# Banded attention and a four-expert MoE on one core: when the routing probabilities are fetched, which engine makes some low halves, and where the last block's B22 lies

## The chip, the cores and the metric

The kernel runs on one core of a Trainium2 chip. A core has a matrix engine (PE; its weight loads are shown as PEld), a vector engine (DVE), a scalar engine (ACT), GpSimd (POOL) and SyncE (SP), which here does nothing but issue DMA transfers. Each engine runs its own instructions in program order and waits for others by semaphores. The metric is the device time of one execution in microseconds; less is better.

## What is computed

Only the shapes and the steps matter here. Half of the eight heads see a plain window of 32 positions, the other half every fourth position in a window of 128. The attention output, 2304 tokens by 512, goes through four experts, whose outputs are weighted by normalised probabilities:

```python
scores = scale * np.matmul(q, k.transpose(0, 1, 3, 2))      # q, k, v: (4, 8, 576, 64)
scores = np.where(masks[None, :, :, :], scores, -1000000000.0)
attn = np.exp(scores - np.max(scores, axis=-1, keepdims=True))
attn = attn / (np.sum(attn, axis=-1, keepdims=True) + 1e-09)
x = np.matmul(attn, v).transpose(0, 2, 1, 3).reshape(B * S, H * D)   # (2304, 512)
p = domain_probs / (domain_probs.sum(-1, keepdims=True) + 1e-09)     # (2304, 4)
for e in range(E):
    h = np.maximum(x @ w1[e], 0.0)           # w1: (4, 512, 1024)
    out += p[:, e:e + 1] * (h @ w2[e])       # w2: (4, 1024, 512)
```

## The kernel before

**Precision.** Every operand of an expert matmul is held as two fp32r tiles, a high half (`hi`, made by ACT, line 113) and a low half (`lo = source - hi`, made by DVE or POOL, line 116); a product is three matmuls, hi·hi, lo·hi and hi·lo (`product`, line 378). In the profile `xh`, `xl` are the halves of x, `g1h`, `g1l`, `g2h`, `g2l` those of w1, `w2h`, `w2l` those of w2, and `hh`, `hl` those of the hidden layer. `r` is a raw weight tile, `xr` raw attention output.

**Attention steps.** `steps` holds 30 attention steps: 12 with one group of queries (a head pair and a third of the sequence), then 18 with two. Iteration n of the main loop (line 702) issues several stages of different steps: the score product of step n (`s_qk`, line 264, tiles `sc`), the max of step n, the exponential of n-1, the sum and the normalisation of n-2 (line 317, POOL), the transpose of n-3 (`pt`, line 329), and the product with v of n-4 (`po`). "Step n" below means this iteration, and its start on PE is told by its score product. The loads of q, k and v for later steps are issued on SP in the same iterations, up to six groups ahead; `q7` below is the q tile of the eighth group, and so on.

**Experts.** A visit (u, m) is one 256-wide slice u of w1 and w2 on block m of 768 tokens. `visits` runs u = 1 to 15 on block 0, then all 16 slices on blocks 1 and 2 in turn. A visit's first product is a Strassen-like scheme with seven products instead of eight (`mm1_a`, `mm1_b`, lines 415 to 448); its operands from x are B11, B21, B22 and four sums of them T1 to T4. `x_sums(i)` (line 199, four DVE subtractions in place in `xr`) makes the sums of the half block i, and `x_part(i, n)` (line 209) splits one operand. `mm2` (line 462) multiplies with w2 and adds to `acc` on DVE. Slice 0 on block 0 is done by `plain` without sums; its X12 lies in the tile that T4 gets afterwards.

**What sets the order.** The order on every engine is the order in the program. Work of preparation (splits, sums) is put into the lists `queue` and `later` by `prepare`, and one item is taken (`step`) after each piece of the experts' generator; `need` takes items until a named one is done. From iteration `START` (14) on, two pieces of the experts' generator are issued in each iteration, and from `OPEN` (20) on twelve.

**Last block.** Block 2 has its own tiles for B11 and B21 only; its other operands lie in tiles of block 0 that are no longer read:

```python
    PLACE = {"T1": "B11", "B22": "B21", "T3": "T2", "T4": "T1"}
```

**Probabilities.** `weigh` (line 643) issues the DMA of the probabilities (`pw<-probs`, 128 partitions by 18 by 4 numbers) at the end of iteration 6 and normalises them with four small DVE instructions; `acc` reads them from the first `mm2` on.

Of the kernel before, what the change touches and what calls it, by code (L numbers as in the profile page):

```python
# [42 lines left out]
def kernel(  # L43
# [11 lines left out]
    nc = tc.nc  # L55
# [22 lines left out]
    pw = const.tile([128, NTT, E], F32, name="pw")  # L78
# [39 lines left out]
    def w1_split(u):  # L118

        r = raw1[u]  # L120
        gh = wp.tile([128, 3, 2, 128], F32R, tag="g1h", name="g1h", bufs=2)
        gl = wp.tile([128, 3, 2, 128], F32R, tag="g1l", name="g1l", bufs=2)
        a11, a12 = r[:, 0:2, 0:128], r[:, 2:4, 0:128]
        a21, a22 = r[:, 0:2, 128:256], r[:, 2:4, 128:256]
        for i, a in enumerate((a11, a12, a22)):
            split(gh[:, i], gl[:, i], a, nc.scalar, nc.gpsimd if u else nc.vector)
            a_op[u, ("A11", "A12", "A22")[i]] = (gh[:, i], gl[:, i])
            yield
        if u == 0:
            gh, gl = (wp.tile([128, 4, FU], F32R, tag=t, name=t) for t in ("g2h", "g2l"))  # L130
            v = (slice(None), slice(0, 2), slice(128, 256))
            split(gh[v], gl[v], a21, nc.scalar, nc.vector)
            a_op[u, "A21"] = (gh[v], gl[v])
            fetch_w1(2)
# [41 lines left out]

    PLACE = {"T1": "B11", "B22": "B21", "T3": "T2", "T4": "T1"}

    def x_op(m, n):
        if (m, n) not in b_op:
# [26 lines left out]
    def x_part(i, n):  # L209


        m, j = divmod(i, 2)
        d = {"T1": "11", "T3": "12", "T2": "22", "T4": "21"}.get(n, n[1:])
        hi, lo = (t[:, :, j * TC:(j + 1) * TC] for t in x_op(m, "T4" if n == "X12" else n))
        split(hi, lo, quarter(i, d), nc.scalar, nc.vector if i == 1 else nc.gpsimd)
        yield


# [282 lines left out]
    def experts(begin):  # L501

        for half in range(2):
            for n in ("X12", "B22") if half else ("B11", "B21"):
                for i in range(2):
                    need(x_part, i, n)
            need(w1_split, 0)
            yield from plain((0, 0), half)
            if half == 1:
                for n in ("T4", "T3", "T1", "T2"):  # L510
                    for j in (1, 0):
                        prepare(x_part, j, n, soon=True)
                prepare(w1_late, 1, soon=True)
                prepare(w1_split, 2)
                prepare(w1_sums, 2)
            need(w2_late, 0)
            yield from mm2((0, 0), True, False, half)
            if half == 0:
                yield from pause("open")
            else:  # L520
                prepare(w2_late, 2)
        need(w1_split, 1)
        yield from mm1_a(visits[0])
        for i, (u, m) in enumerate(visits):
            blocks = [b for v, b in visits if v == u]
            mine = [v for v in visits if v[1] == m]
            ends = m and (u, m) == mine[0], (u, m) == mine[-1]
            if m == blocks[0]:
                need(w1_late, u)
            need_x(m)  # L530
            yield from mm1_b((u, m))
            if m == blocks[-1] and u < LAST:
                prepare(w1_late, u + 1)
            if (u, m) == (NU - 1, 0):
                need(x_sums, 4)
                need(x_sums, 5)
                for n in ("T2", "T1", "T3", "T4"):
                    for j in (4, 5):
                        prepare(x_part, j, n)
            if m == blocks[-1] and u + 2 <= LAST:  # L540
                prepare(w1_split, u + 2)
                prepare(w1_sums, u + 2)
            if m == blocks[0]:
                need(w2_late, u)
            yield from mm2((u, m), *ends, 1)
            if i + 1 < len(visits):
                begin()
                need(w1_split, visits[i + 1][0])
                need_x(visits[i + 1][1], ("B11", "B21"))
                yield from mm1_a(visits[i + 1])  # L550
                if visits[i + 1] == (NU - 1, 0):

                    for j in (4, 5):
                        prepare(x_part, j, "B22")
                    for j in (4, 5):
                        prepare(x_sums, j)
            yield from mm2((u, m), *ends, 0)
            if m == blocks[-1] and u + 2 <= LAST:
                prepare(w2_late, u + 2)
# [27 lines left out]
    with tc.manual_schedule():  # L587
# [38 lines left out]
        def begin():  # L626

            if "over" in gate and "m1" not in gate:
                gate.add("m1")
                early.close()  # L630
                pools["x"] = ctx.enter_context(
                    tc.tile_pool(name="x2", bufs=1, side="right", reuse_waits="tile")
                )
                for n, bufs in ("m1", 2), ("m2", 4):
                    pools[n] = ctx.enter_context(
                        tc.tile_pool(name=n, bufs=bufs, space=psum, reuse_waits="tile")
                    )
                pools["acc"] = pools["x"]
                for n in ("B11", "B21"):
                    for i in (4, 5):  # L640
                        prepare(x_part, i, n)

        def weigh():

            nc.sync.dma_start(out=pw, in_=probs.rearrange("(t p) e -> p t e", p=128))
            nc.vector.reduce_sum(out=ps_, in_=pw, axis=mybir.AxisListType.X)
            nc.vector.tensor_scalar(
                out=ps_, in0=ps_, scalar1=1e-9, scalar2=None, op0=ALU.add
            )
            nc.vector.reciprocal(out=pr_, in_=ps_)  # L650
            nc.vector.tensor_tensor(
                out=pn, in0=pw, in1=pr_.to_broadcast([128, NTT, E]), op=ALU.mult
            )
# [34 lines left out]
        for n, i, names in (  # L688
            (done(*plains[0]), 0, ("B11",)), (done(*plains[0]), 1, ("B11",)),
            (START - 1, 0, ("B21",)), (START - 1, 1, ("B21",)),  # L690
            (done(*dil(0, 1)), 0, ("X12", "B22", None)),
            (OPEN - 1, 1, ("X12", "B22", None)),
            (done(*dil(1, 1, 2)), 2, X_PARTS), (done(*dil(2, 0, 1)), 3, X_PARTS),
        ):
            when.setdefault(n, []).append((i, names))
# [6 lines left out]
        for n in range(len(steps) + LAG):  # L702
# [15 lines left out]
            for i, names in when.get(n, ()):  # L718
                for name in names:
# [1 line left out]
                    if name is None or name == "T2":  # L721
                        prepare(x_sums, i, of=of)
                    if name is not None:
                        prepare(x_part, i, name, of=of)
            if n == 2:
                fetch_w1(0)
                fetch_w2(0)
                fetch_w1(1)
            if n == 4:
                prepare(w1_split, 0)  # L730
                prepare(w2_late, 0)
            if n == 6:
                weigh()
            if n == 8:
                prepare(w1_split, 1)
# [81 lines left out]
```

## Time and profile before

| what | value |
|---|---|
| time, median of 3 runs (lowest to highest) | 878.15 us (878.09 to 879.53) |
| time of the profiled execution | 878.14 us |
| span of its trace, first to last instruction | 876.4 us |
| PE busy | 843.3 us, 96% of the span |
| DVE, POOL, ACT busy | 494.3, 430.3, 328.5 us |
| mean granted clock of PE | 0.986 |

The trace covers the span; 1.74 us of the profiled execution lie outside it. The engine names, the times from the start of the span and the idle time ahead of an instruction (with what ended it, in brackets) are read from the rows further below. A busy PE is not PE at full speed: the granted clock is either 1.0 (2.4 GHz) or 0.5 (1.2 GHz), and a mean between them is a stretch that holds both.

### The profile page before, as it was taken

To read this page: it belongs to the slowest core of one execution; us is meant where nothing else is said; L and a number is where in the kernel's file an instruction comes from. 1 tells how busy PE (TensorE), PEld (TensorE's weight loads), DVE (VectorE), ACT (ScalarE), POOL (GpSimd) and SP (SyncE) were. 2 spreads that over 40 slices of the span, in tenths; PEclk is the share of its full clock that TensorE was granted. 3 is DMA by queue.
4 is the path that set the end of the run, shared out by engine and by line. 5 is a ranking of instruction groups with operands and counts; after the bars stand their busy time and mean duration, and the time that the engine had idled before them with its cause. 6 is when DMAs were issued, how large, how long until landed. Compare 5 with 4: busy or idle time off the path is not lost.

```text
span 876.4 us, 13448 instructions
## 1 busy us (share of the span) xinstructions
PE 843.3 (96%) x5096; PEld 734.6 (84%) x5096; DVE 494.3 (56%) x1029; ACT 328.5 (37%) x771; POOL 430.3 (49%) x508
## 2 busy tenths in 40 slices
PE   8598899999999999899999999999999999999998
PEld 5477678888788988688898988989889898898987
DVE  3577766567565565745555555554555545555454
ACT  4354544445344444433333333422333332343221
POOL 4574887678876677954224323423422432342310
PEclk9699999999999999999999999999999999999999
DMA  7754123322222211230101001001110100100003
GB/s 229 185 161 127 47 87 112 109 83 82 76 62 86 73 49 51 74 117 26 48 25 49 25 25 49 24 25 48 29 44 25 49 24 25 49 25 25 1 25 120
DMA packets 54528, 56.77 MB, mean 65 GB/s; under 512 B 5952, under 2 KB 43840, under 8 KB 54464
## 3 DMA queue, kind: packets, MB, share of 16 engines
q1 hardware_dynamic: 54464, 55.92, 20.7%
q8 instruction: 40, 0.66, 0.3%
q14 instruction: 24, 0.20, 0.1%
HBM read 51.19 MB, written 4.72 MB: 64 GB/s over the span
## 4 chain that ended last, share of the span: by engine, by line
PE 85%; DVE 6%; POOL 5%; issue 1%; ACT 1%; DMA 1%; SPq 0%; POOLq 0%; DVEq 0%; ACTq 0%
PE m L480 42%; PE m1x L382 21%; PE m1y L382 16%; DVE hl L406 3%; PE pt L329 2%; PE sc L264 2%; DVE xr L204 2%; PE po L349 1%; POOL xl_T L116 1%; POOL sm L294 1%; POOL g1l L116 1%; PE wt L675 1%; POOL sm L317 1%; DVE u L442 1%; DMA q_s<-qT 1%
## 5 line engine op out<-in xcount | busy, mean ns | idle before, releaser
L489 DVE SCALAR_TENSOR_TENSOR acc<-m,pn,acc 128x512 f32<-128x512 f32 x270 | 201.9, 749 | 103.1 <-PE m L480 101.7
L480 PE MATMUL m<-w2h,hh 128*128 128x512 f32 x576 | 227.5, 395 | 7.6 <-DVE acc L489 7.1
L480 PE MATMUL m<-w2h,hl 128*128 128x512 f32 x576 | 229.4, 398 | 2.4 <-DVE hl L406 0.9
L116 POOL TENSOR_TENSOR g2l<-r,g2h 128x256 fp32r<-128x256 f32 x124 | 91.7, 761 | 280.0 <-ACT g2h L113 279.9
L480 PE MATMUL m<-w2l,hh 128*128 128x512 f32 x576 | 226.9, 394 | 0.0
L480 PEld LDWEIGHTS m<-w2h,hl 128*128 128x128 f32 x576 | 108.6, 189 | 36.0 <-DVE hl L406 13.6
L480 PEld LDWEIGHTS m<-w2h,hh 128*128 128x128 f32 x576 | 108.7, 189 | 30.9 <-DVE acc L489 10.1
L480 PEld LDWEIGHTS m<-w2l,hh 128*128 128x128 f32 x576 | 108.7, 189 | 20.0
L116 POOL TENSOR_TENSOR w2l<-r,w2h 128x512 fp32r<-128x512 f32 x62 | 80.1, 1309 | 46.0 <-ACT w2h L113 45.6
L438 DVE TENSOR_TENSOR s<-m1x,s 128x384 f32<-128x384 f32 x47 | 26.2, 558 | 109.0 <-PE m1x L382 106.2
L419 ACT ACTIVATE s<-m1x 128x384 f32<-128x384 f32 x47 | 23.1, 491 | 171.4 <-PE m1x L382 171.4
L116 POOL TENSOR_TENSOR g1l<-r,g1h 128x256 fp32r<-128x256 f32 x93 | 69.0, 756 | 35.0 <-ACT g1h L113 34.8
L400 ACT ACTIVATE hh<-s 128x384 fp32r<-128x384 f32 x94 | 49.4, 526 | 97.3 <-DVE s L438 50.8
L431 ACT ACTIVATE u<-m1x 128x384 f32<-128x384 f32 x47 | 23.1, 491 | 149.7 <-PE m1x L382 149.7
L406 DVE SCALAR_TENSOR_TENSOR hl<-s,hh 128x384 fp32r<-128x384 f32 x94 | 59.4, 632 | 30.1 <-ACT hh L400 30.0
L382 PE MATMUL m1x<-xh_T,g2h 128*128 128x384 f32 x188 | 63.8, 339 | 1.5 <-ACT u L431 1.5
L382 PE MATMUL m1x<-xl_T,g2h 128*128 128x384 f32 x188 | 63.4, 337 | 0.0
L382 PE MATMUL m1x<-xh_T,g2l 128*128 128x384 f32 x188 | 63.3, 337 | 0.0
L422 DVE TENSOR_TENSOR s<-m1y,s 128x384 f32<-128x384 f32 x47 | 26.2, 557 | 61.4 <-PE m1y L382 57.1
L113 ACT ACTIVATE g2h<-r 128x256 fp32r<-128x256 f32 x125 | 44.6, 405 | 0.0
L382 PE MATMUL m1y<-xh_B,g2h 128*128 128x384 f32 x128 | 43.0, 336 | 0.0
L382 PE MATMUL m1y<-xl_B,g2h 128*128 128x384 f32 x128 | 42.9, 336 | 0.0
(86 smaller groups left out, 1548.3 us busy)
## 6 DMA issues: line engine op xcount, KB each, us to landing
r<-w SPq DMA_DIRECT2D x64, 512.0 KB, 3.5
v_s<-vw SPq DMA_DIRECT2D x48, 144.0 KB, 3.3
k_s<-kT SPq DMA_DIRECT2D x48, 112.0 KB, 3.2
q_s<-qT SPq DMA_DIRECT2D x48, 96.0 KB, 3.2
out<-acc SPq DMA_DIRECT2D x18, 256.0 KB, 2.1
mask<-masks SPq DMA_DIRECT2D x1, 288.0 KB, 3.2
pw<-probs SPq DMA_DIRECT2D x1, 36.0 KB, 3.3
```

Of the source, the lines that this page charges most:

```text
L113: nc.scalar.activation(out=hi, in_=src, func=AF.Copy)
L116: lo_eng.tensor_tensor(out=lo, in0=src, in1=hi.bitcast(F32), op=ALU.subtract)
L204: nc.vector.tensor_tensor(out=quarter(i, d), in0=quarter(i, a), in1=quarter(i, b), op=ALU.subtract)
L382: nc.tensor.matmul(bank, w[:, k], x[:, k], start=(first and k == 0 and i == 0), stop=(last and k == 1 and i == 2), skip_group_check=True,)
L400: nc.scalar.activation(out=hi, in_=src, func=AF.Relu)
L406: nc.vector.scalar_tensor_tensor(out=lo, in0=src, scalar=0.0, in1=hi.bitcast(F32), op0=ALU.max, op1=ALU.subtract)
L419: nc.scalar.activation(out=s1, in_=x, func=AF.Copy)
L422: nc.vector.tensor_tensor(out=s1, in0=z, in1=s1, op=ALU.add)
L431: nc.scalar.activation(out=u2, in_=x, func=AF.Copy)
L438: nc.vector.tensor_tensor(out=s5, in0=x, in1=s5, op=ALU.add)
L480: nc.tensor.matmul(po, a[:, i * 128:(i + 1) * 128], w, start=(n == 0), stop=(n == 5))
L489: nc.vector.scalar_tensor_tensor(out=acc, in0=po, scalar=pn[:, tt, e:e + 1], in1=acc, op0=ALU.mult, op1=ALU.add,)
```

## The change

1. The DMA of the probabilities moves from the end of iteration 6 to the end of iteration 2, right behind the first three weight loads; the four DVE instructions move to the end of iteration 11.
2. The low halves of w1's slice 1 (three, iterations 8 to 10) go from POOL to DVE.
3. The low halves of x go to DVE for every odd half block (i = 1, 3, 5), where before only i = 1 did.
4. T2, T1 and T3 of half block 0 are queued in iteration 15, ahead of X12 and B22 of half block 1, instead of after `plain`.
5. Block 2 gets a tile of its own for B22. Its T2 lies in block 0's B11 and its T1 in block 0's B21. B11, B21, B22 and the sums of block 2 are queued in `later` as soon as the attention is over, T2 and T1 one visit later, T3 and T4 last.

```diff
-            split(gh[:, i], gl[:, i], a, nc.scalar, nc.gpsimd if u else nc.vector)
+            split(gh[:, i], gl[:, i], a, nc.scalar, nc.gpsimd if u > 1 else nc.vector)
...
-    PLACE = {"T1": "B11", "B22": "B21", "T3": "T2", "T4": "T1"}
+    PLACE = {"T2": "B11", "T1": "B21", "T3": "T2", "T4": "T1"}
...
-        split(hi, lo, quarter(i, d), nc.scalar, nc.vector if i == 1 else nc.gpsimd)
+        split(hi, lo, quarter(i, d), nc.scalar, nc.vector if i % 2 else nc.gpsimd)
...
-                for n in ("T4", "T3", "T1", "T2"):
-                    for j in (1, 0):
+                for n, js in (("T4", (1, 0)), ("T3", (1,)), ("T1", (1,)), ("T2", (1,))):
+                    for j in js:
                         prepare(x_part, j, n, soon=True)
...
             if (u, m) == (NU - 1, 0):
-                need(x_sums, 4)
-                need(x_sums, 5)
-                for n in ("T2", "T1", "T3", "T4"):
+                for n in ("T3", "T4"):
                     for j in (4, 5):
                         prepare(x_part, j, n)
...
                 if visits[i + 1] == (NU - 1, 0):
-                    for j in (4, 5):
-                        prepare(x_part, j, "B22")
-                    for j in (4, 5):
-                        prepare(x_sums, j)
+                    need(x_sums, 5)
+                    for n in ("T2", "T1"):
+                        for j in (4, 5):
+                            prepare(x_part, j, n)
...
-                for n in ("B11", "B21"):
+                for n in ("B11", "B21", "B22"):
                     for i in (4, 5):
-                        prepare(x_part, i, n)
+                        prepare(x_part, i, n, of=later)
+                for i in (4, 5):
+                    prepare(x_sums, i, of=later)
...
-            nc.sync.dma_start(out=pw, in_=probs.rearrange("(t p) e -> p t e", p=128))
             nc.vector.reduce_sum(out=ps_, in_=pw, axis=mybir.AxisListType.X)
...
-            (done(*dil(0, 1)), 0, ("X12", "B22", None)),
+            (done(*dil(0, 1)), 0, ("X12", "B22", None, "t2", "t1", "t3")),
...
-                        prepare(x_part, i, name, of=of)
+                        prepare(x_part, i, name.upper(), of=of)
             if n == 2:
                 fetch_w1(0)
                 fetch_w2(0)
                 fetch_w1(1)
+                nc.sync.dma_start(out=pw, in_=probs.rearrange("(t p) e -> p t e", p=128))
...
-            if n == 6:
+            if n == 11:
                 weigh()
```

PE's instructions keep their order and number; only the names of the tiles that block 2 reads differ. Three places on other engines carry the argument.

On SP, early in the attention, before the change the probabilities stood behind the loads of iteration 6, ahead of the weight tile of slice 2 (`r_465`):

```order
L247 DMA k_s<-kT 128x224
L252 DMA v_s<-vw 96x2x192
L645 DMA pw<-probs 128x18x4
L246 DMA q_s<-qT 128x192
L247 DMA k_s<-kT 128x224
L252 DMA v_s<-vw 96x2x192
L98 DMA r_465<-w 128x4x256
```

With the change they stand behind the three weight loads of iteration 2, ahead of q7 and k7:

```order
L98 DMA r_231<-w 128x4x256
L106 DMA r_233<-w 128x2x512
L98 DMA r_235<-w 128x4x256
L728 DMA pw<-probs 128x18x4
L246 DMA q_s<-qT 128x192
L247 DMA k_s<-kT 128x224
L246 DMA q_s<-qT 128x192
```

So the transfer moved past fourteen loads of q, k and v, which now stand behind it.

On ACT, at the opening of the second half of `plain`, before the change the splits of X12 (`xh_T_0_905`) and B22 (`xh_B_0_919`) of half block 1 came right after an exponential:

```order
L336 ACTIVATE pts<-pt 96x384
L302 ACTIVATE sm_95<-sm_95 128x6x96
L113 ACTIVATE xh_T_0_905<-xr 128x2x192
L113 ACTIVATE xh_B_0_919<-xr 128x2x192
L400 ACTIVATE hh<-m1x 128x384
```

With the change the high halves of T2, T1 and T3 of half block 0 stand ahead of them:

```order
L302 ACTIVATE sm_95<-sm_95 128x6x96
L113 ACTIVATE xh_T_0_1298<-xr 128x2x192
L113 ACTIVATE xh_T_0_1302<-xr 128x2x192
L113 ACTIVATE xh_T_0_1306<-xr 128x2x192
L113 ACTIVATE xh_T_0_905<-xr 128x2x192
L113 ACTIVATE xh_B_0_919<-xr 128x2x192
L400 ACTIVATE hh<-m1x 128x384
```

Their three POOL low halves move likewise, ahead of the four `g2l` of slice 1.

On DVE, in the visits (14, 0) and (15, 0), before the change the eight sums of block 2 stood in one piece behind the hidden layer's low halves and ahead of three additions to `acc`:

```order
L438 TENSOR_TENSOR s_4306<-m1x,s_4306 128x384
L442 TENSOR_TENSOR u_4305<-m1y,u_4305 128x384
L406 SCALAR_TENSOR_TENSOR hl<-s_4306,hh 128x384
L406 SCALAR_TENSOR_TENSOR hl<-u_4305,hh 128x384
L406 SCALAR_TENSOR_TENSOR hl<-m1x,hh 128x384
L204 TENSOR_TENSOR xr<-xr 128x2x192 x8
L489 SCALAR_TENSOR_TENSOR acc_989<-m_4376,pn,acc_989 128x512
```

With the change they stand one visit earlier, one or two at a time between the visit's own instructions, and three low halves of B11, B21 and B22 (`xl_B`) stand just ahead of them on DVE:

```order
L116 TENSOR_TENSOR xl_B_2_4154<-xr,xh_B_2_4153 128x2x192
L204 TENSOR_TENSOR xr<-xr 128x2x192
L438 TENSOR_TENSOR s_4158<-m1x,s_4158 128x384
L204 TENSOR_TENSOR xr<-xr 128x2x192
L442 TENSOR_TENSOR u_4157<-m1y,u_4157 128x384
L406 SCALAR_TENSOR_TENSOR hl<-s_4158,hh 128x384
L406 SCALAR_TENSOR_TENSOR hl<-u_4157,hh 128x384
L204 TENSOR_TENSOR xr<-xr 128x2x192
L406 SCALAR_TENSOR_TENSOR hl<-m1x,hh 128x384
L204 TENSOR_TENSOR xr<-xr 128x2x192
L489 SCALAR_TENSOR_TENSOR acc_989<-m_4219,pn,acc_989 128x512
```

The sums are spread, and two of them now stand ahead of the hidden layer's work in this visit.

## Rows read from the trace of the kernel before

**Rows 1.** Timeline of PE: start us, us, instruction, idle before and its releaser.
```profile
29.62 0.87 PE L329 MATMUL pt<-ident,sm 128*96 128x128 f32 x3 [7.68 <-POOL sm L317]
...
75.40 0.44 PE L382 MATMUL m1x<-xh_T,g1h 128*128 128x384 f32 x1 [1.15 <-ACT xh_T L113]
...
229.32 0.50 PE L480 MATMUL m<-w2h,hh 128*128 128x512 f32 x1 [1.53 <-DVE acc L489]
...
369.02 0.79 PE L480 MATMUL m<-w2h,hh 128*128 128x512 f32 x1 [3.64 <-DVE acc L489]
```

**Rows 2.** Timeline of DVE around the probabilities (columns as above).
```profile
26.83 0.23 DVE L646 TENSOR_REDUCE ps__69<-pw 128x18 f32<-128x72 f32 x1 [6.65 <-DMA pw<-probs]
...
28.09 0.45 DVE L310 TENSOR_REDUCE su<-sm 128x3 f32<-128x291 f32 x1
...
29.23 0.61 DVE L116 TENSOR_TENSOR g2l<-r,g2h 128x256 fp32r<-128x256 f32 x1
```

**Rows 3.** Timeline of PE: score products of steps 7, 13 and 14.
```profile
20.51 0.71 PE L264 MATMUL sc<-k_s,q_s 64*64 64x96 f32 x12
...
44.07 0.73 PE L264 MATMUL sc<-k_s,q_s 64*64 64x96 f32 x24
...
47.45 1.24 PE L264 MATMUL sc<-k_s,q_s 64*64 64x96 f32 x24
```

**Rows 4.** Tile k_s, the one transfer (k7) issued at 13.04 us.
```profile
DMA to landing us min/median/max: 6.9/6.9/6.9
```

**Rows 5.** Windows: busy us of PE, PEld, DVE, ACT, POOL; clock; DMA share, GB/s.
```profile
25.00:26.50 1.50, 0.00 (x0) 0.00 (x0) 0.00 (x0) 0.00 (x0) 0.00 (x0) 0.50 0.92 48
47.50:51.00 3.50, 3.50 (x33) 3.28 (x33) 2.47 (x15) 1.88 (x5) 3.07 (x3) 0.53 0.47 131
333.50:348.90 15.40, 15.40 (x79) 13.96 (x78) 8.15 (x13) 7.58 (x18) 12.73 (x16) 1.00 0.11 35
```

**Rows 6.** Groups by line of DVE, 26 to 36 us: busy us, mean ns.
```profile
L116 DVE TENSOR_TENSOR w2l<-r,w2h 128x512 fp32r<-128x512 f32 x2 | 1.8, 918 | 0.0
```

**Rows 7.** Waits of SP's queue, 0 to 45 us: total us, times, longest.
```profile
SPq L98 <- DVE g2l L116: 2.9, 1, 2.9
...
SPq L252 <- DMA r<-w: 1.3, 1, 1.3
```

**Rows 8.** Timeline of SP: issues of v5, q12, w1 slice 2, k15.
```profile
19.40 0.57 SPq L252 DMA_DIRECT2D v_s<-vw  x1
...
24.16 1.62 SPq L246 DMA_DIRECT2D q_s<-qT  x1
...
29.87 0.38 SPq L98 DMA_DIRECT2D r<-w  x1
...
36.34 0.42 SPq L247 DMA_DIRECT2D k_s<-kT  x1
```

**Rows 9.** Tile k_s, the one transfer (k15) issued at 36.34 us.
```profile
DMA to landing us min/median/max: 3.9/3.9/3.9
```

**Rows 10.** Timeline of ACT: four high halves of x in a row.
```profile
90.18 1.75 ACT L113 ACTIVATE xh_T<-xr 128x384 fp32r<-128x384 f32 x4
```

**Rows 11.** Waits of all engines, 97 to 102 us: total us, times, longest.
```profile
PE m L480 <- DVE hl L406: 0.7, 2, 0.4
```

**Rows 12.** Timeline of POOL: an attention step's subtraction behind low halves.
```profile
225.74 1.15 POOL L294 TENSOR_TENSOR sm<-sm,nm 128x576 f32<-128x576 f32 x1
```

**Rows 13.** Timeline of DVE: `s` of visit (14, 0); the eight sums of block 2.
```profile
339.61 0.56 DVE L438 TENSOR_TENSOR s<-m1x,s 128x384 f32<-128x384 f32 x1 [2.46 <-PE m1x L382]
...
358.97 9.33 DVE L204 TENSOR_TENSOR xr<-xr 128x384 f32<-128x384 f32 x8
```

**Rows 14.** Critical chain, merged: start us, us, what.
```profile
369.02 5.49 PE m L480 x12
...
396.26 4.12 PE m L480 x18
```

**Rows 15.** Line 204, all sums: duration ns min/median/max.
```profile
L204 DVE TENSOR_TENSOR xr<-xr x24: 543/964/1534, 61.2 to 367.3; 128x384 f32<-128x384 f32 x24
```

## The prediction

> **What bounds the kernel.** PE is busy for 96% of the span and the change leaves its instructions as they are, so I add up nothing but time in which PE stood still or ran at the lower clock. The timeline of PE gives the idle places. The largest is 7.68 us ahead of a transpose in step 8 and the next 3.64 us ahead of an `mm2` of block 0; smaller ones lie where `plain` opens its second half and near 229 us [rows 1]. For each the reader should ask which instruction came last, and follow that engine's own timeline back.
>
> The first one is a wait for data. DVE stood 6.65 us for `pw<-probs`, with the sums of the next attention step queued behind [rows 2]; POOL's normalisation and PE's transpose followed. Steps 7 to 14 therefore took from 20.51 to 47.45 us, 26.94 us [rows 3].
>
> **The change part by part.**
>
> *Probabilities.* The wait goes, since by iteration 11 the transfer has long landed. What is late next? Three things.
>
> First, k7. The transfer now stands ahead of it, in a queue that was already slow: k7 landed 6.9 us after its issue at 13.04, at 19.9 us [rows 4], 0.6 us before step 7 used it. The probabilities come in runs of 16 bytes. In the 1.5 us from 25.0 the DMA engines were 0.92 busy and moved 48 GB/s, 72 KB, of which the probabilities are 36 [rows 5]. Between half of that stretch and all of it, 0.7 to 1.5 us, is their price; I take 1.3, as the rate shows them to fill most of it. k7 then lands at 21.2, and step 7 starts at about 21.3 instead of 20.5.
>
> Second, DVE. A step's own work there is 1.14 us, from its sum at 28.09 to the next low half at 29.23 [rows 2]; five steps, 7 to 11, make 5.7. Added in these steps are two `w2l` at 0.92 [rows 6], so 1.8; one `g2l` and the three `g1l` that come over from POOL at no more than 0.61 each, 2.4; and the four normalising instructions with one more `g1l`, 26.83 to 28.09, 1.3 [rows 2]. Together 11.2 us, and step 12 starts at 32.5. If all of it were hidden, the steps would go at PE's pace. The row nearest to that is step 13 to 14, 3.4 us with two groups, or 1.7 for one [rows 3]; five make 8.5, and step 12 starts at 29.8. I take the sum, because DVE is in order and every step needs its reciprocal.
>
> Third, SP. v5 is the eighth transfer behind w1's slice 1, and its issue at 19.40 waited 1.3 us for a weight load [rows 7, 8]; I read this as at most eight transfers in flight. With the change v5 is the eighth behind the probabilities, so it waits until these land, at about 20.6, 1.2 us later than before, with every later load behind it. Slice 2 of w1 was ready to be issued at 29.87 less a wait of 2.9 for its buffer [rows 7, 8], at 27.0; with the change DVE frees that buffer in time. Add 1.2; take off the probabilities' own issue, 0.6, and the 1.1 us by which q12 behind them was slower than a common issue (1.62 against 0.57) [rows 8]: 26.5. From there to the landing of k15 it took 6.5 us of issues and 3.9 us of transfer [rows 8, 9], so k15 lands at 36.9. Step 13 needs it; the engines would be there by 32.5 plus at most 3.4, 35.9. So the loads bind: step 13 at 36.9, step 14 one spacing of 3.4 later, at 40.3 instead of 47.45. **Gain 7.2 us.** Without this bind it is 8.2; with DVE's work hidden too, 10.9. Step 14 ran at clock 0.53 for 3.5 us [rows 5], which cost some 1.6 us; PE has as many gaps ahead of it with the change, so I leave that as it is, and take 5 us as the lower end (price of the probabilities 0.2 more, and another slow stretch of 1.6 us or so).
>
> *T2, T1 and T3 of half block 0 earlier.* ACT has three high halves more ahead of X12, at 0.44 each [rows 10], 1.3 us. PE had been waiting for just that one, 1.15 us [rows 1]. PE's first two matmuls need no low half and cover a little of DVE's; I take a loss of 1.2 us. Later the same three are missing where ACT, DVE and POOL are crowded, at 88 to 102 us; but the chain there (sum, high half, four splits, copy on ACT) keeps its length, and I count only the two waits for `hl`, 0.7 us [rows 11], since POOL comes to the attention's subtraction earlier. **Loss 0.5 us**; from a loss of 1.2 to a gain of 1.
>
> *Low halves of half block 3 on DVE.* The wait of 1.53 us at 229.32 [rows 1] ends a chain: POOL got to the attention step's subtraction at 225.74 only [rows 12], behind low halves; ACT's exponential and `hh` behind it were late, and so `hl` and `acc`. POOL loses seven instructions ahead of it, so the wait goes. DVE takes them, between its additions. **Gain 1.5 us**, 0 to 2.
>
> *Last block.* The eight sums held DVE for 9.33 us, 1.17 each [rows 13], with three `acc` queued behind; PE ran out of PSUM and stood 3.64 us [rows 1], and then its twelve matmuls took 5.49 us, where eighteen take 4.12 at full clock [rows 14], so 2.75: 2.7 lost to the clock. Both go, 6.3 us. In their place stand eleven DVE instructions in visit (14, 0). Before, DVE was busy there for 8.15 of 15.40 us, PE without a gap [rows 5]. A sum takes 0.54 us at least and 0.96 in the median [rows 15]. At 0.54 eleven take 5.9 and fit into the 7.2 us that are free; at 1.17 they take 12.9, and 5.6 us do not fit. POOL is at work for 12.73 of the 15.40 us [rows 5], and so I price them by the slow row.
>
> The excess is not all PE's. Only the instructions that stand ahead of `s`, `u` and the first `hl` hold it back; those behind delay `acc`, for which four PSUM tiles give slack, and `s` of the next visit, whose `hl` is needed ten us later. Counting along the order: ahead of `s` now stand three low halves and a sum, 3.8 us at the median price and 4.7 at the slow one. `s` had 2.46 us of idle time right ahead of it [rows 13], and between the additions DVE had about one more (an estimate out of the 7.2): `s` is 0.3 to 1.2 late, I take 0.8. One sum more, 1.2, stands ahead of `u` and the two `hl`. PE waits some 2.0 us in two or three pieces, all short. **Gain 4.3 us**; from -0.3 (all the excess, and one us more) to 6.3.
>
> The row shows 1.17 for a sum beside a busy POOL against 0.54 at best [rows 13, 15]. The Trainium skill, "SBUF — State Buffer", section "Who interferes with whom", says that a DVE instruction with two SBUF inputs and a GpSimd instruction that reads SBUF exclude each other for the whole of the earlier one's time; the trace agrees with alternation. By it the moved low halves would cost DVE a POOL instruction's time each, which speaks against this part of the change, and the sum would be that of the third rival below.
>
> *The rest.* The tile of its own for B22 and the new places cost nothing that I can see: block 0's B11 and B21 are last read in the visit before T2 and T1 are written, and PE's order is the same. If T2 came late, PE would wait in visit (16, 2), over 25 us later; that is its cover.
>
> **Sum.** 7.2 - 0.5 + 1.5 + 4.3 = 12.5 us. The profiled execution took 878.14 us, 1.74 of it outside the span, and equals the median (878.15): 878.1 - 12.5 = 865.6 us. Its own range is 862 to 869.
>
> **The rivals.**
>
> *The loads do not bind.* If eight in flight is a misreading, or the issues catch up, the early gain is 8.2 to 10.9. For it: SP had idle time before most of these loads. Against it: the landings above. 864.6 to 861.9 us, some 862.5.
>
> *DVE is too full.* In the last block all 5.6 us of the excess reach PE, and the three `hl` there slow down by 0.5 each: 6.3 less 7.1, -0.8. The early part and the rest stay: 878.1 - 7.2 + 0.5 - 1.5 + 0.8 = 870.7. For it: 1.17 in the row; against: `acc` has slack.
>
> *The stall only moves.* The step that loses its wait starves for q and k in steps 8 to 13, and 3 of 7.2 us remain: 869.8. For it: 0.6 us of slack at k7. If nothing at all were left of the early gain (the change doesn't do what it says), 872.8.
>
> *Slower.* Each moved instruction costs what the worst sum did, 1.53 us [rows 15]: eleven make 16.8 in visit (14, 0), 9.6 more than fit, and with `hl` 11 us and a new slow stretch of 2.7; seven make 10.7 near 215 us and cost 4 instead of gaining 1.5. Then 878.1 - 7.2 + 0.5 + (11 + 2.7 - 6.3) + 4 = 882.8. It decides once DVE costs PE over 14 us in both places together (the early gain, and the two waits that go). Against it: that price occurred once in 24.
>
> **How the numbers follow.** My forecast 0.55; loads do not bind 0.17; DVE too full 0.15; the stall only moves 0.09, slower 0.03; 0.01 is left. The range 861 to 871 takes in the first, most of the second, half of the third and most of the fourth (0.55, 0.15, 0.08, 0.07), 0.85; cut at 869 it would leave out 0.3. About 0.2% (1.8 us) is what a measurement of this kernel can tell from no change. Faster by more than that: the first four, 0.95; same 0.02; slower 0.03.
>
> **What would show it.** In the profile after: no wait of DVE for the probabilities; step 7 near 21.3 and step 14 near 40.3; the issue of v5 right after the probabilities land, and step 13 starting as k15 lands (a wait for a load at PE, or none, decides between forecast and first rival). A longer wait for `xh_T` where `plain` opens its second half. No wait near the old 229. No slow clock after visit (14, 0), but waits of PE for `hl` in it, 2 us in all; over 5 us there would be the third case. I am wrong if PE's idle time early in the attention is as long as before, or if a new stretch at the lower clock shows up.

## The result, and the profile after

| what | before | after |
|---|---|---|
| median time (lowest to highest), 4 executions each | 878.12 us (876.96 to 879.53) | 868.04 us (866.52 to 869.99) |
| ratio to before, 95% interval | | 0.9886 (0.986 to 0.9911) |
| profiled execution: span | 876.4 us | 866.9 us |
| mean granted clock of the executions | 0.986 (profiled) | 0.987 to 0.995 |

The change gained 10.1 us where 12.5 were forecast; the time lies inside the range. PE executes the same 5096 matmuls in the same order in both kernels, so the start of the k-th matmul in one trace less its start in the other says how much is **in hand** at that place. Step 12's score product, for example, began at 41.33 us before and at 34.17 after: 7.2 us in hand. The table gives this at eleven places, named by their time in the trace of before.

| place, us before | 20.5 (step 7) | 41.3 (step 12) | 47.5 (step 14) | 74 | 88 | 115 | 130 | 324 | 365 | 393 | end |
|---|---|---|---|---|---|---|---|---|---|---|---|
| in hand, us | -1.5 | 7.2 | 5.6 | 5.5 | 1.2 | 3.5 | 3.0 | 3.8 | 2.6 | 9.2 | 9.5 |

The wait of 7.68 us is gone, but two stretches give back what it brought: steps 13 and 14, and the ten microseconds behind 74. The timeline of PE after (columns as in [rows 1, 3]) has the places:

```profile
17.50 0.57 PE L349 MATMUL po<-pts,v_s 96*64 96x64 f32 x12 [2.26 <-ACT pts L336]
...
22.03 1.17 PE L264 MATMUL sc<-k_s,q_s 64*64 64x96 f32 x12
...
34.17 0.73 PE L264 MATMUL sc<-k_s,q_s 64*64 64x96 f32 x24
...
36.91 0.38 PE L264 MATMUL sc<-k_s,q_s 64*64 64x96 f32 x4
...
39.33 0.71 PE L264 MATMUL sc<-k_s,q_s 64*64 64x96 f32 x20 [2.04 <-DMA k_s<-kT]
...
41.86 1.24 PE L264 MATMUL sc<-k_s,q_s 64*64 64x96 f32 x24
...
71.11 0.69 PE L382 MATMUL m1x<-xh_T,g1h 128*128 128x384 f32 x1 [2.39 <-ACT xh_T L113]
...
216.07 0.49 PE L480 MATMUL m<-w2h,hh 128*128 128x512 f32 x1 [0.80 <-DVE acc L489]
...
225.57 0.50 PE L480 MATMUL m<-w2h,hh 128*128 128x512 f32 x1 [0.33 <-DVE acc L489]
...
337.66 0.44 PE L382 MATMUL m1x<-xh_T,g1h 128*128 128x384 f32 x1 [0.92 <-DVE s L438]
```

Step 7 starts at 22.03 and its product takes 1.17 us, the duration of the lower clock. Step 13 starts at 36.91, does four matmuls and waits 2.04 us for k15. Where `plain` opens its second half the wait for `xh_T` has grown from 1.15 [rows 1] to 2.39 us. In the last block nothing is left of the 3.64 us of [rows 1]; 0.92 us ahead of `s` is new.

SP's timeline after shows why the loads are late (issues of the probabilities, q7, v5 and k15; columns: start, duration of the issue):

```profile
12.47 0.51 SPq L728 DMA_DIRECT2D pw<-probs  x1
13.08 5.97 SPq L246 DMA_DIRECT2D q_s<-qT  x1
...
22.38 0.57 SPq L252 DMA_DIRECT2D v_s<-vw  x1
...
33.96 0.42 SPq L247 DMA_DIRECT2D k_s<-kT  x1
```

Right behind the probabilities one issue takes 5.97 us, where a common one takes about half a microsecond [rows 8]. SP does not wait for a landing here, it stands inside the issue, and everything behind starts from 19.05. (The view of SP's waits puts 5.0 us of it down to PE's product with v at 17.50; but in `contig` below, with the same order on PE, this issue was through at 14.6, ahead of that product, so it is no wait for PE.) The tile view of k15 (`k_s`, issued at 33.96) puts its landing at 39.2:

```profile
DMA to landing us min/median/max: 5.2/5.2/5.2
```

And in the windows of after (columns as in [rows 5]) the clock is low at 40 to 47 and at 70 to 78 us, and full behind the last block's old wait:

```profile
40.00:47.00 7.00, 7.00 (x54) 5.87 (x52) 5.47 (x30) 3.63 (x8) 5.64 (x5) 0.51 0.68 190
70.00:78.00 8.00, 6.36 (x20) 5.86 (x21) 5.45 (x8) 1.48 (x4) 3.45 (x3) 0.57 0.23 63
330.00:345.00 15.00, 14.03 (x70) 12.09 (x69) 14.06 (x20) 7.34 (x19) 14.58 (x15) 1.00 0.12 37
366.00:376.00 10.00, 9.94 (x50) 8.47 (x49) 6.88 (x10) 3.96 (x9) 7.81 (x10) 1.00 0.38 130
```

### The profile page after: what moved, and what is told of

Same layout as the page of the kernel before. It is cut to its first block, busy times and chain, and to the rows that moved or that the text cites. A ratio compares the mean times of both kernels' runs of the same rounds, so it can differ in the third digit from the quotient of the medians.

```text
span 866.9 us, 13453 instructions
## 1 busy us (share of the span) xinstructions
PE 842.7 (97%) x5096; PEld 734.4 (85%) x5096; DVE 503.9 (58%) x1046; ACT 328.7 (38%) x771; POOL 417.6 (48%) x491
## 4 chain that ended last, share of the span: by engine, by line
PE 87%; DVE 6%; POOL 2%; ACT 2%; DMA 2%; issue 1%; SPq 0%; POOLq 0%; DVEq 0%; ACTq 0%
PE m L480 44%; PE m1x L382 22%; PE m1y L382 17%; DVE hl L406 2%; PE sc L264 1%; PE pt L329 1%; PE po L349 1%; DVE xr L204 1%; PE wt L674 1%; DVE sm L278 1%; DVE u L442 1%; DMA r<-w 1%; DMA k_s<-kT 1%; ACT hh L400 1%; POOL xl_T L116 0%
## 5 line engine op out<-in xcount | busy, mean ns | idle before, releaser
L116 POOL TENSOR_TENSOR g1l<-r,g1h 128x256 fp32r<-128x256 f32 x90 | 66.7, 756 | 36.4 <-ACT g1h L113 36.4
L382 PE MATMUL m1x<-xh_T,g2h 128*128 128x384 f32 x156 | 52.8, 339 | 0.6 <-ACT u L431 0.3
L382 PE MATMUL m1x<-xl_T,g2h 128*128 128x384 f32 x156 | 52.5, 337 | 0.2 <-DVE xl_T L116 0.2
L382 PE MATMUL m1x<-xh_T,g2l 128*128 128x384 f32 x156 | 52.3, 335 | 0.0
```

The source lines that it names most:

```text
L116: lo_eng.tensor_tensor(out=lo, in0=src, in1=hi.bitcast(F32), op=ALU.subtract)
L382: nc.tensor.matmul(bank, w[:, k], x[:, k], start=(first and k == 0 and i == 0), stop=(last and k == 1 and i == 2), skip_group_check=True,)
```

## The experiments

All times are medians of 4 to 6 executions, ratios are to the kernel before on the same chip. One program's executions differ by 1 to 5 us, and go with their mean granted clock: `warm` below took 865.25 us at 0.998 and 870.06 at 0.986. A time alone therefore settles little under 2 us; the traces are read for the places. Four theories were at stake: that part 4 costs the clock at 71 to 77 us (A), that the probabilities' many runs hold SP (B), that the clock and not the wait is what part 4 costs (C), and that an old wait for w1's load starts the lower clock of the early attention (D).

**Parts alone or undone.** `late_t` undoes part 4 in the changed kernel:

```diff
-            (done(*dil(0, 1)), 0, ("X12", "B22", None, "t2", "t1", "t3")),
+            (done(*dil(0, 1)), 0, ("X12", "B22", None)),
...
-                for n, js in (("T4", (1, 0)), ("T3", (1,)), ("T1", (1,)), ("T2", (1,))):
-                    for j in js:
+                for n in ("T4", "T3", "T1", "T2"):
+                    for j in (1, 0):
```

> The changed kernel with part 4 undone: T2, T1 and T3 of half block 0 are queued after plain again. Theory A: the three high halves ahead of X12 make PE wait 2.39 instead of 1.15 us at 71 us, and with that its clock falls to 0.5 until 77; of the 5.5 us in hand at 70 us only 3.2 are left at 118. Undone: wait about 1.2 us, clock 1.0 from 71 to 77, 5.0 to 5.5 us in hand there and 1 to 2 of them lost again at 86 to 98, where the waits of before return. Time 864.5 to 866.5 us. Rival: the lower clock has to do with the earlier arrival of the whole stretch (DVE, POOL and loads in another phase), not with part 4; then it stays and the time is 868 to 869 us.

Measured 867.81 us, 0.9878 (0.9863 to 0.9893): like the changed kernel. In its windows the stretch at 70 to 78 us is at full clock, as theory A said, but a new one stands at 88 to 95, behind the two waits in the PE rows below it:

```profile
24.00:43.00 19.00, 19.00 (x200) 13.43 (x200) 11.36 (x64) 9.12 (x24) 11.74 (x16) 0.50 0.84 238
70.00:78.00 8.00, 5.74 (x43) 4.62 (x36) 6.05 (x22) 3.27 (x8) 1.78 (x3) 1.00 0.29 75
88.00:95.00 7.00, 6.27 (x60) 5.13 (x60) 3.49 (x6) 3.69 (x10) 6.92 (x8) 0.52 0.00 0
```

```profile
85.93 0.41 PE L382 MATMUL m1y<-xh_T,g2h 128*128 128x384 f32 x1 [0.98 <-DVE s L422]
...
88.73 0.69 PE L382 MATMUL m1x<-xh_T,g2h 128*128 128x384 f32 x1 [1.52 <-ACT u L431]
```

Part 4 shortens these two waits (to 0.48 and 0.31 us in the trace of after) and lengthens one at 71; each way one piece at half clock is paid. From 74 to 115 us `late_t` lost 1.0 us of what it had in hand, the changed kernel 2.1. The first window shows a second thing: here PE ran at half clock from 24 to 43 us without a gap (19.00 of 19.00 us busy), and only 3.4 us were in hand at step 14.

`probs_alone` is the kernel before with part 1 alone:

```diff
-            nc.sync.dma_start(out=pw, in_=probs.rearrange("(t p) e -> p t e", p=128))
             nc.vector.reduce_sum(out=ps_, in_=pw, axis=mybir.AxisListType.X)
...
                 fetch_w1(1)
+                nc.sync.dma_start(out=pw, in_=probs.rearrange("(t p) e -> p t e", p=128))
...
-            if n == 6:
+            if n == 11:
```

> The kernel before with part 1 alone (fetched in iteration 2, normalised in iteration 11). If the early gain belongs to part 1 alone: step 14 at 41.5 to 42 us, 5.5 us in hand at 70 us, no clock of 0.5 from 71 to 77 (theory A), waits at 86 to 98, 229 and 369 us as before: 872 to 873 us. Rival: the stretch at 0.5 comes with the earlier arrival and not with part 4: 875 to 876 us.

Measured 872.89 us, 0.9941 (0.9927 to 0.9955), so 5.2 us for part 1. Both readings were half right: no low clock at 71 to 77, but the one at 88 to 95 (0.52), as in `late_t`. In hand at 74 us were 4.2, at 115 us 3.2. In the last block the wait stood as before, in this PE row, but the clock stayed at 1.00 behind it, as the window says, where it fell to half before ([rows 14]: 5.49 us for twelve):

```profile
366.17 0.50 PE L480 MATMUL m<-w2h,hh 128*128 128x512 f32 x1 [3.60 <-DVE acc L489]
```

```profile
366.00:376.00 10.00, 9.68 (x47) 8.27 (x47) 7.58 (x13) 6.43 (x15) 9.31 (x11) 1.00 0.78 262
```

`last_alone` is the kernel before with part 5 and the low halves of half block 5 on DVE (`i in (1, 5)`).

> The kernel before with part 5 alone and the low halves of half block 5 on DVE; everything up to 330 us as before. If the gain of the last block is independent of the rest: wait of 3.64 us and the lower clock at 369 us gone, waits of about 1.5 us for s and hl in visit (14, 0), net 5 us: 873 to 873.5 us. By the prediction 4.3 us: 874. Rival: part of it depended on the other parts (POOL freed of low halves): 875 us or more.

Measured 874.23 us, 0.9955 (0.9941 to 0.9969), 4.0 us; in its trace, which is of its fastest execution (872.43 us), nothing was in hand at 324 us, -1.1 at 365, 5.6 at 393. The gain does not need the other parts. Its cost is the wait for `s`:

```profile
341.39 0.44 PE L382 MATMUL m1x<-xh_T,g1h 128*128 128x384 f32 x1 [0.92 <-DVE s L438]
```

`half3_pool` puts only the low halves of half block 3 back on POOL (`i in (1, 5)` for `i % 2` in the changed kernel).

> The changed kernel with the low halves of half block 3 on POOL again (those of half block 5 stay on DVE). As predicted, 1.5 us are lost by it: 869.5 us. By the trace of the changed kernel the wait at 229 shrank from 1.53 to 0.33 us, but one of 0.8 came at 216 where there had been 0.25, so 0.6 us: 868.6 us. Rival: it is neutral, 868.0 us.

Measured 870.82 us, 0.9907 (0.9891 to 0.9924). The intervals overlap, the early clock differs too, and the trace is of its fastest execution (868.43 us), so I go by the place: from 130 to 324 us the changed kernel wins 0.8 us and this one 0.1. Its waits are those of before:

```profile
214.62 0.51 PE L480 MATMUL m<-w2h,hh 128*128 128x512 f32 x1 [0.24 <-DVE acc L489]
...
225.33 0.50 PE L480 MATMUL m<-w2h,hh 128*128 128x512 f32 x1 [1.52 <-DVE acc L489]
```

`p2_pool` puts the low halves of w1's slice 1 back on POOL (`u > 1` to `u`).

> The changed kernel with the low halves of w1's slice 1 on POOL again. By the prediction DVE's own work sets the pace of steps 7 to 12, and the three low halves are 1.8 us of it; k15 binds behind it: step 12 about 1.5 us earlier than 34.2, steps 13 and 14 where they are, time unchanged at 868 us. Rival: POOL sets the pace (PE's waits in these steps are for its normalisation): steps 8 to 12 are later by 1 to 2 us, and the time is 868.5 to 869.5 us.

Measured 870.05 us, 0.9901 (0.9886 to 0.9915). Inconclusive: PE ran at half clock here without a gap, so neither DVE nor POOL set the pace, as this window shows:

```profile
20.00:38.00 18.00, 18.00 (x167) 12.79 (x164) 9.39 (x53) 9.23 (x25) 11.86 (x18) 0.50 0.85 239
```

**SP and the probabilities.** `fetch_4` moves the fetch, the DMA line alone, from `n == 2` to the end of iteration 4.

> The changed kernel with the probabilities' DMA at the end of iteration 4 instead of 2, the normalisation stays in iteration 11. Theory B: behind three weight loads that are still in flight the transfer of 2304 runs of 16 bytes holds SP, whose next issue took 5.97 us, and so k7, step 7 and at last k15 are late. In iteration 4 the weights have nearly landed: no issue over 2 us, step 7 at about 20.5 instead of 22.0 us, k15 lands at 37 to 38 instead of 39.2, and the time is 1 to 2 us less, 866 to 867 us. Rival: the same bytes and runs stand ahead of the later loads in any case; SP catches up by step 13, k15 lands at 39 and the time stays at 868 us.

Measured 867.07 us, 0.9867 (0.9854 to 0.9881). SP's rows:

```profile
20.20 0.60 SPq L729 DMA_DIRECT2D pw<-probs  x1
20.89 1.22 SPq L246 DMA_DIRECT2D q_s<-qT  x1
```

The issue behind it takes 1.22 us, PE waits for a load only once, 0.45 us, and 6.1 us are in hand at step 14. Step 7 was not earlier (22.87): PE's clock was already low there, behind a wait of 2.21 us at 17.7 for ACT.

`contig` leaves the fetch in iteration 2 and changes the layout in memory only:

```diff
-                nc.sync.dma_start(out=pw, in_=probs.rearrange("(t p) e -> p t e", p=128))
+                nc.sync.dma_start(out=pw, in_=probs)
...
-        "probs": moe_domain_probs[rows], "w1": moe_w1, "w2": moe_w2,
+        "probs": moe_domain_probs[rows].reshape(-1, 128, E).transpose(1, 0, 2), "w1": moe_w1, "w2": moe_w2,
```

> The changed kernel with one thing different: the probabilities lie in memory partition by partition, so that the same 36 KB come as 128 runs of 288 bytes instead of 2304 runs of 16; place and time of the fetch are those of the changed kernel. Theory B (the number of runs holds SP): the next issue takes under 1.5 us instead of 5.97, k7 lands near 20 us, no wait of PE for a load at 20 to 24 us, k15 lands 1 to 2 us earlier than 39.2; 866 to 867 us. Rival (three weight loads of 512 KB hold the queue whatever stands behind them): the next issue still takes 5 to 6 us and the time stays at 868 us.

Measured 868.07 us, 0.9882 (0.987 to 0.9895). On SP the rival falls:

```profile
12.45 1.57 SPq L728 DMA_DIRECT2D pw<-probs  x1
14.12 0.51 SPq L246 DMA_DIRECT2D q_s<-qT  x1
```

0.51 us in place of 5.97: the number of runs held SP, behind the same three weight loads. The other traces repeat it: the issue behind the probabilities took 4.71 to 6.54 us in the six kernels that fetch 2304 runs in iteration 2, and 0.38 to 0.75 in the four that fetch 128. k15 was issued at 31.21 and landed 5.0 later, at 36.2; step 14 began at 40.49, with 7.0 us in hand. The Trainium skill, "DMA: Bandwidth & Descriptors", section "Rules for kernel authors", says that a last dimension that is not contiguous becomes one descriptor per element, and advises rearranging it. Here the last dimension was contiguous, for 16 bytes, so that advice does not reach this case; the trace shows that short runs cost the queue too. Yet the median did not move. In hand at 115 us were 4.9, behind the same stretch at half clock from 69 to 77 us.

**The clock.** `warm` gives PE work where it stood still:

```diff
             need(w1_split, 0)
+            if half == 1:
+                dummies(20)
             yield from plain((0, 0), half)
```

> The changed kernel with twenty extra matmuls (bf16, 256 columns, into a PSUM tile that nothing reads) ahead of the second half of plain, where PE stood still for 2.39 us at 68.7 to 71.1. They compute nothing of the result. Theory C: the wait for xh_T itself costs only 1.2 us more than before, and the rest of what is lost from 70 to 78 us (another 2.5 to 3) is the lower clock that follows it; with PE at work in the wait the clock stays at 1.0, the first product of the half starts at the same 71.1, and 2 to 3 us are gained: 865 to 866 us. Rival: the clock falls in spite of it (the stretch ahead is busy enough to lower it), or falls some us later, at the waits near 87 us: 868 us.

Its PE rows and the window around the place:

```profile
67.42 3.33 PE L676 MATMUL wt<-ident 128*128 128x256 bf16 x20
70.50 0.42 PE L382 MATMUL m1x<-xh_T,g1h 128*128 128x384 f32 x1
```

```profile
69.00:77.00 8.00, 7.11 (x39) 5.52 (x37) 6.80 (x9) 3.14 (x8) 3.81 (x4) 1.00 0.14 38
```

The clock stays at 1.0, and nothing falls later: from 74 to 115 us 0.2 us are won where the changed kernel lost 2.1. So theory C holds for this place, and the other traces bear it out: all six kernels with part 4 and without these matmuls have the wait of 2.39 us and a stretch at half clock behind it, and lose 1.2 to 2.3 us from 74 to 115; the four with them have no such stretch and win 0.2. The median, 868.29 us, 0.9883 (0.9867 to 0.99), does not show it: the profiled execution took 865.25 us at a mean clock of 0.998, the four others 867.0 to 870.1 at 0.986 to 0.992. Where these lost theirs isn't in a trace; in the other kernels' traces the place that varies most is 17 to 50 us.

`split6` takes away the wait that seemed to start that early stretch, in `contig`:

```diff
-            if n == 4:
+            if n == 6:
                 prepare(w1_split, 0)
                 prepare(w2_late, 0)
```

> The kernel with the probabilities in 128 runs, and the splits of w1's and w2's slice 0 queued in iteration 6 instead of 4. Theory D: in all kernels so far ACT stands some 3 us for w1's load (g1h, landing at 16 to 17.5 us) ahead of an attention step's copy, PE waits 1.0 to 3.0 us for it at 17 us, and that wait starts the lower clock at 18 to 24 us, in some executions to 38; whether it does is what makes the executions of one kernel differ by 3 us. Without the wait: no idle of PE over 0.7 us at 17, clock 1.0 from 16 to 36, step 7 at 20 us or earlier; median 865.5 to 867 us, mean clock of the executions 0.991 or more. Rival: the splits come later and hold DVE in steps 9 to 12, or the clock falls there for another wait: 868 us, mean clocks as before.

Measured 870.16 us, 0.9912 (0.9898 to 0.9926). Theory D falls in its consequence: the wait at 17 us is gone, but PE then overtakes the loads, and at the opening of `plain` it waits for a high half of x, which on ACT stands behind an exponential that had itself waited 1.61 us for POOL:

```profile
19.87 1.14 PE L264 MATMUL sc<-k_s,q_s 64*64 64x96 f32 x12 [1.65 <-DMA k_s<-kT]
...
42.90 0.44 PE L382 MATMUL m1x<-xh_B,g1h 128*128 128x384 f32 x1 [2.44 <-ACT xh_B L113]
```

Each is followed by a stretch at half clock; 9.8 us were in hand near 38 us and 5.0 at 58.

`combo` adds the extra matmuls to `split6`.

> The kernel with all three: probabilities in 128 runs, splits of slice 0 in iteration 6, and twenty extra matmuls ahead of the second half of plain (they compute nothing of the result). If the two stretches at the lower clock (17 to 40 us, 70 to 78 us) are what is lost of the early gain, both are gone: clock 1.0 up to 100 us but for some 3 us near 42, 7 to 8 us in hand at 118 us, mean clock 0.995 or more in every execution, 862 to 864 us. Rival: a stretch at the lower clock appears elsewhere in its place (87 to 95 us): 866 to 868 us.

Measured 868.52 us, 0.9891 (0.9874 to 0.9908): the rival in kind, at other places than it named. The clock was at 1.0 from 70 to 78 us, but at 0.57 from 32 to 40 and 0.53 from 43 to 50. Against `split6` it is 1.6 us less, with intervals that overlap.

`contig_warm` and `f4_warm` keep the splits in iteration 4 and combine the extra matmuls with either remedy for SP.

> The changed kernel with the probabilities in 128 runs and the twenty extra matmuls (they compute nothing of the result); the splits stay in iteration 4. If the two gains add up (k15 some 3 us earlier, no lower clock at 70 to 78 us): 7 us in hand at 70 us and 6.5 at 118, a span of about 862.5 us and a median of 864 to 866 us. Rival (what is gained in one place is lost at the next, as the two runs before showed): 867 to 868.5 us.

> The changed kernel with the fetch in iteration 4 and the twenty extra matmuls (they compute nothing of the result). Fetch in iteration 4 alone gave 867.1 us with mean clocks of 0.990 to 0.992 in every execution, of which the stretch at 70 to 78 us is part; without that stretch 864.5 to 866 us. Rival: 867 us or more, because the stretch comes later or the clock of the early attention varies more than it did in those four executions.

`contig_warm` took 867.98 us, 0.9876 (0.9861 to 0.9892); `f4_warm` 865.44 us (864.71 to 865.93), 0.9851 (0.9838 to 0.9865), the best here, with mean clocks of 0.994 to 0.997 in all five executions. Against the same kernels without the extra matmuls that is no gain for `contig_warm` (`contig` 868.07) and 1.6 us for `f4_warm` (`fetch_4` 867.07, the intervals overlap). In its trace the early steps run at full clock until the loads stop PE, and only then the clock falls, as its PE row and windows show:

```profile
38.03 1.22 PE L264 MATMUL sc<-k_s,q_s 64*64 64x96 f32 x20 [2.81 <-DMA k_s<-kT]
```

```profile
24.00:38.00 14.00, 8.73 (x131) 6.08 (x131) 9.29 (x50) 7.48 (x19) 11.43 (x16) 1.00 0.85 252
38.00:45.00 7.00, 6.97 (x69) 5.84 (x70) 4.94 (x28) 3.53 (x8) 4.97 (x5) 0.52 0.69 182
...
69.00:77.00 8.00, 7.09 (x38) 5.57 (x38) 6.67 (x9) 3.00 (x8) 3.79 (x5) 1.00 0.14 39
```

9.2 us were in hand at step 12 and 6.3 at step 14: with SP's stop away, the loads of q and k are what the early steps run into. That its executions agree better than `contig_warm`'s was measured; why, no run tells.

## Why the prediction was right, and where its terms were off

The range held the time and the sign was right; the forecast was 2.4 us too good. The two large terms are shown by parts: part 1 alone gave 5.2 us and part 5 alone 4.0, together 9.2 of the 10.1. Part 4 gave nothing that the times show (`late_t`), and what part 2 is worth is not shown.

Yet one of the two signs by which the prediction called itself wrong did come: "a new stretch at the lower clock shows up". One stands at 70 to 78 us, where before had none, and the one near 47 us is twice as long. And the sum is nearer than its terms: the terms of the early attention, of T2, T1 and T3 and of half block 3 were forecast too well by 1.7, 1.6 and 0.7 us, the second of them beyond its own range, while the last block is better than forecast by 1.2. That these set each other off in part is luck. The terms, from the table of what is in hand:

| term | forecast | measured in the trace |
|---|---|---|
| early attention, to 74 us | 7.2 | 5.5 (3.9 to 6.8 in the four kernels that are the same up to there) |
| T2, T1 and T3 earlier, 74 to 115 us | -0.5 | -2.1 |
| 115 to 130 us | none | -0.5 (short waits for `hh` and `hl`, 0.16 and 0.36 us, near 118) |
| half block 3, 130 to 324 us | 1.5 | 0.8 |
| last block, 324 to 393 us | 4.3 | 5.5 (-1.2, then 6.7) |
| rest | none | 0.3 |
| sum | 12.5 | 9.5 (spans 876.4 and 866.9) |

**Early attention.** "The loads bind" was right: step 13 waits for k15, which landed at 39.2 and not 36.9. Two steps ahead of it failed. The first is the cost of the probabilities on SP. I took their own issue, 0.6 us, and a delay of 1.2 for v5; SP stood 5.97 us in the next issue instead, v5 went out at 22.38 and not 20.6, slice 2 at 28.85 and not 26.5, and k15 at 33.96 and not 33.0. `contig` shows that the number of runs did it: with 128 instead of 2304 that issue takes 0.51 us, and k15 goes out at 31.21. The second is k15's own transfer, 3.9 us by the row of before: it took 5.2, and 5.0 in `contig` as well, which is 1.3 of the 2.3 us; why is open. From the landing to step 14 it then took 2.7 us, not 3.4.

The late load does not by itself make the term smaller. `warm`, the same program up to 68 us, had SP's stop too (5.30 us) and k15 at 38.76, yet 6.7 us in hand at step 14, since its clock stayed at full speed behind that wait, as its PE row and window show:

```profile
38.89 0.71 PE L264 MATMUL sc<-k_s,q_s 64*64 64x96 f32 x20 [1.21 <-DMA k_s<-kT]
```

```profile
42.00:69.00 27.00, 25.95 (x372) 20.17 (x371) 22.58 (x113) 13.87 (x34) 20.65 (x20) 1.00 0.72 196
```

k7's landing (21.35, forecast 21.2) came out right through two errors, since it was issued six microseconds later and took 2.3 us instead of 6.9. The reading of at most eight in flight was not refuted: SP's queue waited for weight loads for 2.6 us in all in `contig`, and not once in the changed kernel, where the long issue had outlasted them. The pace of steps 7 to 12, 12.1 us by the PE rows against 11.2, was near, though I can't say that it is DVE's: most of PE's waits there are for POOL's normalisation, and `p2_pool` didn't tell them apart.

**The clock.** "I leave that as it is" cost most of this term, by the comparison with `warm`, and is the next step that failed. At 40 to 47 us the stretch at 0.51 is twice as long as that of [rows 5] at 47.5 to 51. Among the four kernels that are the same up to there, how long PE runs at half clock from 18 to 47 us goes with what is in hand at step 14, from 3.4 (`late_t`, half clock from 24 to 43) to 6.7 us (`warm`, half clock only near 24 to 28). What decides it no run tells.

**T2, T1 and T3.** ACT's four high halves in a row made PE wait 1.24 us more, as priced (1.2). What I did not see is that the clock falls behind that wait. `warm` shows it: the wait filled, the loss of 2.1 becomes a gain of 0.2. And `late_t` shows the other side: without part 4 a stretch at half clock stands at 88 to 95 instead. So the place was right and the clock behind it was left out of the sum; the loss lies outside the term's own range, whose end was 1.2.

**Half block 3.** The wait at 229 shrank from 1.53 to 0.33 us, but one at 216 grew to 0.80, where `half3_pool` and before have about 0.24. DVE got seven instructions and `acc` came late once: half the forecast, within its bounds.

**Last block.** Here the working came out step by step. DVE's rows in visit (14, 0) after show three low halves and one sum ahead of `s`, as counted, the third low half and what follows it being:

```profile
334.95 1.17 DVE L116 TENSOR_TENSOR xl_B<-xr,xh_B 128x384 fp32r<-128x384 f32 x1 [0.85 <-ACT xh_B L113]
336.05 1.09 DVE L204 TENSOR_TENSOR xr<-xr 128x384 f32<-128x384 f32 x1
337.06 0.55 DVE L438 TENSOR_TENSOR s<-m1x,s 128x384 f32<-128x384 f32 x1
337.52 0.61 DVE L204 TENSOR_TENSOR xr<-xr 128x384 f32<-128x384 f32 x1
```

`s` is late by 0.92 us (forecast 0.8), and PE loses 1.2 us there instead of 2.0. "DVE is too full", which the prediction also calls the third rival, did not happen, though DVE was busy for 14.06 of 15.00 us and POOL for 14.58: the sums there took 0.61 to 1.09 us each, not the slow 1.17. By the rule of the Trainium skill, "SBUF — State Buffer", section "Who interferes with whom", that the prediction weighed, each would pay a POOL instruction's time; the trace does not bear out that price, since the sums took 0.07 to 0.55 us more than the 0.54 of the fastest [rows 15], and POOL's instructions there 0.74 us or more. Of the 6.3 us that I let go, 3.64 are the wait; the 2.7 of lower clock did not follow that wait in `probs_alone`, so they are a gain over the profiled execution of before, not one that the wait always costs; without them 2.8 of the 5.5 us would be left, an estimate from these rows.

**Other rivals.** "The loads do not bind" falls with PE's row at 39.33; "slower" was nowhere near. "The stall only moves" named the right kind of wait, a load in these steps, but 5.5 of the gain stayed, not 3.

## What to carry to other kernels

When a stall is removed, the next wait in line decides what stays: here a load, then a wait for ACT, each followed by PE at half clock. Cost a moved transfer by what it does to the queue that issues it (number of runs, what is in flight ahead of it), not by its bytes alone; laying the table out so that each partition reads one run took 4.4 us off its own issue and the next here, though nothing off the median. Where a wait can't be removed, spare matmuls in it can keep the clock, which in the traces was worth 1.4 to 2.5 us from 74 to 115 us, no less than the 1.24 us by which the wait had grown; in the medians two of the four pairs show 1.6 us, with intervals that overlap, and two show nothing.

## What the runs showed of the hardware that was not expected

- An issue on SP can last: behind 36 KB in runs of 16 bytes, with three loads of 512 KB ahead, the next took 5.97 us; with nothing but the layout changed, 0.51; with the 16-byte runs issued eight microseconds later, 1.22.
- The length of one wait does not tell whether the clock falls behind it. It stayed at 1.00 after 3.60 us (`probs_alone`, 366 us) and was half after 3.64 at the same place before; 0.98 and 1.52 us in a row brought 0.52 in `late_t`, while before, with 0.98 and 1.51, it was 1.00 throughout 88 to 95 us:

```profile
89.86 0.41 PE L382 MATMUL m1y<-xh_T,g2h 128*128 128x384 f32 x1 [0.98 <-DVE s L422]
...
92.66 0.44 PE L382 MATMUL m1x<-xh_T,g2h 128*128 128x384 f32 x1 [1.51 <-ACT u L431]
```

```profile
88.00:95.00 7.00, 4.51 (x44) 3.58 (x43) 5.33 (x7) 4.13 (x12) 5.07 (x6) 1.00 0.23 71
```

- At half clock PE can be the bound itself: it was busy for 19.00 of 19.00 us in `late_t` from 24 to 43 us and for 18.00 of 18.00 in `p2_pool`, where at full clock it had waits for POOL, ACT and loads.
